# A query weight loaded in 16 + 112 partitions, and the final wait put ahead of the branch, in a decode kernel

## The chip, the core and the metric

The kernel runs on one core of a Trainium2 chip. What is measured is the time of one execution on the device, in microseconds (us), and the median of several executions counts. For the kernel before, three runs gave 1286.26, 1286.32 and 1286.26 us.

## What is computed

One token passes a block with attention and a feed-forward network side by side. Both start from the same normalized input, and both results are added to the input.

```python
xn = _layernorm(x)                                   # x: 1 x 1 x 640
q  = (xn @ wq).reshape(1, 1, 32, 128)                # wq: 640 x 4096
scores = einsum("bhqd,bhkd->bhqk", q, k) * 128**-0.5 # k, v: 1 x 32 x 32768 x 128
o  = einsum("bhqk,bhkd->bhqd", softmax(scores), v)
A  = o.reshape(1, 1, 4096) @ wo                      # wo: 4096 x 640
B  = (silu(xn @ w_gate) * (xn @ w_up)) @ w_down      # hidden width 1728
return x + A + B
```

All inputs are bfloat16. The caches of keys and values hold 32 heads with 32,768 positions of 128 numbers each, 8.39 MB for each of the 64 tensors (K and V of each head); they make up nearly all of the 554 MB that the kernel reads.

## The kernel before

**Buffers.** SBUF holds a ring of three slots, each 64 KB in every partition (`ring`, `SLOTS = 3`). The units of work pass through it in a fixed order: wq, K of head 0, K of head 1, V of head 0, K of head 2, V of head 1, and so on, V of head 31 last, then the feed-forward weights, then wo. Unit number n uses slot n mod 3. So wq lies in slot 0, K of heads 0 and 1 in slots 1 and 2, and V of head 0 is the first unit that takes a slot over, wq's.

**Loads.** All large loads are issued by SyncE (lines 231 to 253). Each has 128 partitions as its rows: partition p takes the p-th contiguous piece of the tensor in HBM, 65,536 bytes for K or V and 40,960 bytes for wq. Before SyncE issues a load into a slot that was used, it waits until the engine that reads the slot is done: L231 and L240 wait for TensorE's work on the unit before. SyncE is a queue in program order. A load's semaphore rises by 16 when all of it has landed.

**The start.** The helper `ahead` moves an instruction that was just added to the program's first basic block in front of the drain that its engine executes ahead of the entry barrier. It's used for wq (SyncE, L158) and for the row x (ScalarE, L159), so that these two loads are issued before the engines pass the barrier and branch to their own blocks. In their blocks, TensorE and VectorE work out the layernorm (lines 286 to 295 and 538 to 558) and leave the normalized input, repeated over 128 columns, in `xnb`. TensorE then waits for `xnb` and for wq (L297 and L298) and computes q for all heads with 40 matrix products (L301). ScalarE copies q to SBUF (L485). SyncE waits for TensorE's eight q steps ahead of V of head 0.

**The main part.** For each head VectorE multiplies K by q in place (L577), TensorE sums the products in groups (L310), VectorE reduces and finds the maximum, ScalarE takes the exponential (L503), and TensorE multiplies the weights by V (L342, L358). The work on V of one head lies between steps of the next head.

**The end.** The last V and wo come in pieces with a semaphore each. TensorE multiplies by the gate, up, down and wo weights (L424, L435, L451), VectorE and TensorE turn the result into 20 rows of 32 numbers (`orow`), and SyncE, having waited for `s_fin`, stores it (L256). After the store, SyncE leaves its block: it branches to the program's final basic block. `body.close()` at the end of the function creates that block; the next line empties it of what the block's exit put there, and L648 then puts one instruction into it, SyncE's wait for the store's semaphore `s_out`. So SyncE branches while the store is under way, and waits after that.

Of the kernel before, what the change touches and what calls it, by code (L numbers as in the profile page):

```python
# [12 lines left out]
def bass_parallel_sum__gqa_block_cached__swiglu_ffn__decode_kernel(  # L13
# [18 lines left out]
    NCD = D // 128  # L32
# [47 lines left out]
    with ExitStack() as es:  # L80
# [3 lines left out]
        def sem(name):  # L84
            return es.enter_context(nc.semaphore(name))
# [34 lines left out]
        s_x, s_wq, s_out = sem("x"), sem("wq"), sem("o")  # L120
# [18 lines left out]
        wq = flat[:, WQ_S * CE:WQ_S * CE + NCD * H * DH]  # L139
# [7 lines left out]
        def ahead(start):  # L147

            at_start = nc.main_func.blocks[0]
            n = len(at_start.instructions)  # L150
            start()
            ins = list(at_start.instructions)
            new = ins[n:]
            drain = next(i for i, x in enumerate(ins)
                         if x.engine == new[0].engine and type(x).__name__ == "InstDrain")
            at_start.instructions = ins[:drain] + new + ins[drain:n]

        ahead(lambda: nc.sync.dma_start(wq, A_wq.rearrange("(p c) n -> p (c n)", c=NCD)).then_inc(s_wq, 16))  # L158
        ahead(lambda: nc.scalar.dma_start(xrow, A_x[0, 0:1, :]).then_inc(s_x, 16))  # L159
        body = ExitStack()  # L160
        block = body.enter_context(nc.Block(no_gpsimd_drain=True))
        f0 = FFN_S * CE
        wg = flat[:, f0:f0 + NCD * F]
        wu = flat[:, f0 + NCD * F:f0 + 2 * NCD * F]
# [22 lines left out]
        def kv_src(cache, h, j0, n):  # L187
            return cache[0, h].rearrange("(p j) d -> p (j d)", p=128)[:, j0 * DH:(j0 + n) * DH]
# [20 lines left out]
        with nc.psum_tensor("ps8", [128, 8, 512], F32) as ps8:  # L209
# [11 lines left out]
            @block.sync  # L221
            def sp(e):
                owner = {}
                for u in units:
                    s = slot_of[u]
                    if s in owner:
                        e.wait_ge(*owner.pop(s))
                    if u[0] == "wq":
                        owner[s] = (s_q, NQB)
                    elif u[0] == "k":  # L230
                        e.dma_start(ring[:, s, :], kv_src(A_k_cache, u[1], 0, NJ)).then_inc(s_slot[s], 16)  # L231
                        owner[s] = (s_qk, NHF * (u[1] + 1))
                    elif u == LASTV:
                        j = 0
                        for i, n in enumerate(TAIL):
                            e.dma_start(ring[:, s, j * DH:(j + n) * DH],
                                        kv_src(A_v_cache, u[1], j, n)).then_inc(s_tail[i], 16)
                            j += n
                    elif u[0] == "v":
                        e.dma_start(ring[:, s, :], kv_src(A_v_cache, u[1], 0, NJ)).then_inc(s_slot[s], 16)  # L240
                        owner[s] = (s_pv, u[1] + 1)
                    elif u[0] == "ffn":
                        e.dma_start(wg, B_w_gate.rearrange("(p c) n -> p (c n)", c=NCD)).then_inc(s_ffn[0], 16)
                        e.dma_start(wu, B_w_up.rearrange("(p c) n -> p (c n)", c=NCD)).then_inc(s_ffn[1], 16)
                        e.dma_start(flat[:, d0:d0 + FM * D], B_w_down[0:FM * 128, :].rearrange(
                            "(p j) n -> p (j n)", j=FM)).then_inc(s_ffn[2], 16)
                        e.dma_start(wdr, B_w_down[FM * 128:F, :].rearrange(
                            "f (t n) -> (f t) n", t=2)).then_inc(s_ffn[2], 16)
                    else:
                        wo_src = A_wo.rearrange("(p j) n -> p (j n)", j=OC)  # L250
                        j = 0
                        for i, n in enumerate(WTAIL):
                            e.dma_start(wo[:, j * D:(j + n) * D], wo_src[:, j * D:(j + n) * D]).then_inc(s_wo[i], 16)  # L253
                            j += n
                e.wait_ge(s_fin, 2)
                e.dma_start(out[0, 0:1, :].rearrange("o (r m) -> (o r) m", m=32), orow[:, :]).then_inc(s_out, 16)  # L256

            @block.gpsimd
            def pool(g):
# [21 lines left out]
            def pe(t):  # L281
# [13 lines left out]
                t.matmul(misc[:, 1:2], lhsT=ones[:, :], rhs=st[:, 2:3], start=True, stop=True).then_inc(s_pa, 1)  # L295

                t.wait_ge(s_a, 11)  # L297
                t.wait_ge(s_wq, 16)  # L298
                with t.Fori(0, NQB) as b:
                    for c in range(NCD):  # L300
                        mm = t.matmul(banks[:, bass.ds(b * 512, 512)], lhsT=xnb[:, c, :],  # L301
# [341 lines left out]
                v.wait_ge(s_or, 1)  # L643
                v.tensor_copy(out=orow[:, :], in_=orow_ps).then_inc(s_fin, 1)

        body.close()
        nc.main_func.blocks[-1].instructions = []
        nc.sync.wait_ge(s_out, 16)  # L648


# [26 lines left out]
```

## Time and profile before

| quantity | value |
|---|---|
| median of three runs | 1286.26 us |
| the profiled execution | 1286.26 us |
| its span, first to last instruction | 1284.9 us |
| mean granted TensorE clock | 0.889 |
| TensorE matrix products busy | 1042.9 us, 81% |
| VectorE busy | 672.2 us, 52% |
| ScalarE busy | 52.1 us, 4% |
| bytes read from HBM | 553.99 MB |
| bytes over the span | 431 GB/s |

The span runs from the issue of wq at 0.00 us to the end of the final wait at 1284.9 us; the 1.36 us between the span and the execution's time lie outside of the instructions that the profile records. "Busy" is the time in which an engine executes instructions, and the DMA's share is the mean over the core's 16 DMA engines. In the timeline a line gives the start in us, the duration in us, the engine (SPq is SyncE's queue, PE TensorE, DVE VectorE, ACT ScalarE), the source line, the operation, and in brackets the idle time ahead of it with what ended it. For a DMA the duration is the time of issuing it; when it lands is told in the table of DMA issues. The trace also records every single DMA packet, here one for each row of a load, with its start, its duration and its bytes.

### The profile page before, as it was taken

The numbers are of one execution on the slowest core, as the hardware profiler recorded it, in microseconds if no ns is written. First come the engines' busy times: TensorE is split into PE (matmuls) and PEld (weight loads), VectorE is DVE, ScalarE is ACT, GpSimd is POOL, SyncE is SP. The second block draws the span as 40 slices with busy tenths as digits, with TensorE's granted clock in tenths as the row PEclk, the third lists the DMA queues.
The fourth block names the chain that finished last, engine by engine and source line by source line (L and its number), as shares of the span: only waits on it lengthen the run. The fifth ranks groups of instructions, "written<-read, shape, count | busy, mean of one in ns | idle before, by whom it ended". The sixth has DMA issues, their size and how long they took to land.

```text
span 1284.9 us, 10032 instructions
## 1 busy us (share of the span) xinstructions
PE 1042.9 (81%) x5160; PEld 261.2 (20%) x3240; DVE 672.2 (52%) x409; ACT 52.1 (4%) x139; POOL 2.6 (0%) x18
## 2 busy tenths in 40 slices
PE   3599777789787798778798877898787798778797
PEld 1021112221112221112221112221112221112227
DVE  0855665445664446664446664446654446654451
ACT  2000000000000000000000000000000000000000
POOL 0000000000000000000000000000000000000000
PEclk9799888898888898888998888998888998888995
DMA  9999999999999999999999999999999999999998
GB/s 424 424 441 433 430 431 441 428 433 433 437 433 428 445 426 435 428 441 428 433 443 428 433 430 441 428 433 435 435 433 430 443 426 435 433 437 433 428 427 370
DMA packets 10987, 554.16 MB, mean 431 GB/s; under 512 B 1247, under 2 KB 1504, under 8 KB 1760
## 3 DMA queue, kind: packets, MB, share of 16 engines
q1 hardware_dynamic: 10974, 554.00, 99.8%
q8 instruction: 9, 0.15, 0.0%
q14 instruction: 2, 0.02, 0.0%
q10 hardware_dynamic: 2, 0.00, 0.0%
HBM read 553.99 MB, written 0.00 MB: 431 GB/s over the span
## 4 chain that ended last, share of the span: by engine, by line
DMA 53%; PE 29%; DVE 12%; issue 5%; SPq 0%; DVEq 0%
DMA ring<-in_A_k_cache_dram 51%; PE ps L358 16%; DVE ring L577 12%; PE ps L310 10%; DMA ring<-in_A_wo_dram 2%; PE ps L342 1%; PE ps L329 1%; PE ps L400 0%; PE ps L394 0%; PE ps L388 0%; PE ps L451 0%; SPq L253 0%; DVEq L577 0%; DVE sc L583 0%; DVE pmax L589 0%
## 5 line engine op out<-in xcount | busy, mean ns | idle before, releaser
L577 DVE TENSOR_TENSOR ring<-ring,qb 128x8192 bf16<-128x8192 bf16 x128 | 557.8, 4421 | 314.9 <-DMA ring<-in_A_k_cache_dram 314.9
L310 PE MATMUL ps<-ring,ident 128*128 128x512 bf16 x1920 | 499.6, 419 | 0.0
L358 PE MATMUL ps<-ring,P 128*4 128x512 bf16 x1920 | 429.0, 379 | 0.0
L329 PE MATMUL ps<-ring,ident 128*128 128x512 bf16 x128 | 56.1, 439 | 218.5 <-DVE ring L577 217.9
L358 PEld LDWEIGHTS ps<-ring,P 128*4 128x4 bf16 x1920 | 158.2, 85 | 230.1
L329 PEld LDWEIGHTS ps<-ring,ident 128*128 128x128 bf16 x128 | 12.6, 99 | 617.0 <-DVE ring L577 357.3
L583 DVE TENSOR_REDUCE sc<-ps 128x64 f32<-128x512 f32 x128 | 82.3, 685 | 64.0 <-PE ps L310 64.0
L595 DVE TENSOR_SCALAR negb<-ps 128x1 f32<-128x1 f32 x32 | 5.1, 159 | 108.4 <-PE ps L400 108.4
L503 ACT ACTIVATE P<-sc,negb 128x256 bf16<-128x256 f32 x32 | 16.2, 507 | 957.2 <-DVE negb L595 957.2
L592 DVE TENSOR_REDUCE m<-ps 1x1 f32<-1x128 f32 x32 | 8.9, 278 | 85.2 <-PE ps L394 85.2
L380 PEld LDWEIGHTS ps<-identf,o 4*128 4x128 f32 x248 | 30.7, 190 | 13.1 <-issue 13.1
L380 PE MATMUL ps<-identf,o 4*128 4x1 f32 x248 | 33.3, 251 | 0.0
L388 PEld LDWEIGHTS ps<-rsum,ones 128*128 128x128 f32 x64 | 12.1, 190 | 100.1 <-issue 99.2
L494 ACT ACTIVATE o<-ps,rzb 4x512 f32<-4x512 f32 x31 | 21.0, 677 | 6.3 <-PE ps L345 6.3
L301 PE MATMUL ps<-ring 128*128 x40 | 10.3, 425 | 11.4 <-DMA ring<-in_A_wq_dram 11.4
L499 ACT ACTIVATE ocol<-ps 128x1 f32 (+1 forms) x31 | 5.4, 173 | 222.4 <-PE ps L380 222.4
L342 PE MATMUL ps<-ring,P 128*4 x64 | 14.3, 379 | 0.0
L589 DVE TENSOR_REDUCE pmax<-sc 128x1 f32<-128x256 f32 x32 | 13.4, 420 | 0.0
L394 PE MATMUL ps<-identf,pmax 128*1 128x128 f32 x64 | 12.2, 272 | 1.2 <-DVE pmax L589 1.2
L400 PE MATMUL ps<-m,ones 1*128 1x1 f32 x64 | 12.1, 256 | 0.4 <-DVE m L592 0.4
L400 PEld LDWEIGHTS ps<-m,ones 1*128 1x128 f32 x64 | 9.4, 183 | 14.0 <-issue 13.3
L565 DVE RECIPROCAL rzb<-ps 128x1 f32<-128x1 f32 x32 | 5.1, 158 | 8.1 <-PE ps L388 8.1
(75 smaller groups left out, 97.2 us busy)
## 6 DMA issues: line engine op xcount, KB each, us to landing
ring<-in_A_v_cache_dram SPq DMA_DIRECT2D x2, 4096.0 KB, 36.5
ring<-in_A_wq_dram SPq DMA_DIRECT2D x1, 5120.0 KB, 15.6
ring<-in_A_wo_dram SPq DMA_DIRECT2D x3, 1280.0 KB, 24.2
ring<-in_B_w_gate_dram SPq DMA_DIRECT2D x1, 2160.0 KB, 22.6
ring<-in_B_w_up_dram SPq DMA_DIRECT2D x1, 2160.0 KB, 27.5
ring<-in_B_w_down_dram SPq DMA_DIRECT2D x1, 2080.0 KB, 31.2
ring<-in_A_wo_dram SPq DMA_DIRECT2D x1, 800.0 KB, 28.3
ring<-in_A_k_cache_dram SPq DMA_DIRECT2D x32, 41.5
```

The lines of the kernel that those rows point to most:

```text
L310: return t.add_instruction(mybir.InstMatmult(start_tensor_calc=False, stop_tensor_calc=stop, tile_size=(128, 128), tile_position=(0, 0), l ...
L329: t.matmul(ob, lhsT=ident[:, :], rhs=src, start=True, stop=False)
L342: t.matmul(O, lhsT=P[:, h % PR, bass.ds(b * (RUN * W) + j, W)], rhs=flat[:, bass.ds(b * (RUN * W * DH) + (s * CE + j * DH), W * DH)], star ...
L358: mm = t.matmul(O, lhsT=P[:, h % PR, j:j + W], rhs=ring[:, s, j * DH:(j + W) * DH], start=(j == 0), stop=(j + W == NJ))
L380: mm = t.matmul(fold_ps, lhsT=o4[:, m * DH:(m + 1) * DH], rhs=identf[0:W, m:m + 1], start=(m == 0), stop=(m == W - 1))
L394: t.matmul(misc[0:1, 0:128], lhsT=pmax[:, h % SR:h % SR + 1], rhs=identf[:, :], start=True, stop=True).then_inc(s_t, 1)
L400: t.matmul(misc[:, 128:129], lhsT=ones[0:1, :], rhs=m1[0:1, h % SR:h % SR + 1], start=True, stop=True).then_inc(s_b, 1)
L494: a.activation(out=o4[:, :], in_=O, func=ACTF.Copy, scale=rzb[0:W, h % SR:h % SR + 1]).then_inc(s_o4, 1)
L503: a.activation(out=P[:, h % PR, :], in_=sc[:, :], func=ACTF.Exp, bias=negb[:, h % SR:h % SR + 1], scale=c_scale, accum_out=rsum[:, h % SR: ...
L577: v.tensor_tensor(out=kh, in0=kh, in1=q[:, None, :].to_broadcast([128, HF, DH]), op=ALU.mult).then_inc(s_mul, 1)
L583: v.tensor_reduce(out=sc[:, i * HF:(i + 1) * HF], in_=bank[i].rearrange("p (j e) -> p j e", e=G), axis=AX.X, op=ALU.add).then_inc(s_red, 1)
L589: v.tensor_reduce(out=pmax[:, h % SR:h % SR + 1], in_=sc[:, :], axis=AX.X, op=ALU.max).then_inc(s_max, 1)
```

## The change

The change has two parts. The first: wq is loaded with two DMAs in place of one, partitions 0 to 15 and partitions 16 to 127, both ahead of the entry barrier and both on SyncE's queue with the same semaphore, so that TensorE waits for 32 in place of 16. The second: SyncE's wait for the output store is moved from the final block to the end of SyncE's own block, so that SyncE waits first and branches afterwards; the final block is then left empty.

```diff
-        ahead(lambda: nc.sync.dma_start(wq, A_wq.rearrange("(p c) n -> p (c n)", c=NCD)).then_inc(s_wq, 16))
+        wq_src = A_wq.rearrange("(p c) n -> p (c n)", c=NCD)
+        for a, b in ((0, 16), (16, 128)):
+            ahead(lambda: nc.sync.dma_start(wq[a:b, :], wq_src[a:b, :]).then_inc(s_wq, 16))
         ahead(lambda: nc.scalar.dma_start(xrow, A_x[0, 0:1, :]).then_inc(s_x, 16))
-        body = ExitStack()
-        block = body.enter_context(nc.Block(no_gpsimd_drain=True))
+        block = es.enter_context(nc.Block(no_gpsimd_drain=True))
...
                 e.dma_start(out[0, 0:1, :].rearrange("o (r m) -> (o r) m", m=32), orow[:, :]).then_inc(s_out, 16)
+                e.wait_ge(s_out, 16)
...
                 t.wait_ge(s_a, 11)
-                t.wait_ge(s_wq, 16)
+                t.wait_ge(s_wq, 32)
...
-        body.close()
-        nc.main_func.blocks[-1].instructions = []
-        nc.sync.wait_ge(s_out, 16)
+    nc.main_func.blocks[-1].instructions = []
```

## The prediction

> **What bounds the kernel now.** I read the page's queue and DMA lines first, then the table of DMA issues, the SyncE waits, and last the timeline of the start and of the end, because the change touches only these two places.
>
> The page, transfers:
> ```profile
> DMA packets 10987, 554.16 MB, mean 431 GB/s; under 512 B 1247, under 2 KB 1504, under 8 KB 1760
> ...
> q1 hardware_dynamic: 10974, 554.00, 99.8%
> ```
> SyncE's queue keeps the 16 DMA engines busy for 99.8% of the span. The trace's packet records say how: a 40,960 B row of wq takes 1.514 us and a 65,536 B row of K or V 2.42 us on its engine, 27.05 GB/s in both, and 16 x 27.05 = 433 GB/s. 554.00 MB / 16 / 27.05 GB/s = 1280.0 us of the 1284.9 us span. So each DMA engine is a full line of work; a microsecond that an engine loses anywhere is not won back later.
>
> The page, issues (KB each where it is the same, us from issue to landing):
> ```profile
> ring<-in_A_wq_dram SPq DMA_DIRECT2D x1, 5120.0 KB, 15.6
> ...
> ring<-in_A_k_cache_dram SPq DMA_DIRECT2D x32, 41.5
> ring<-in_A_v_cache_dram SPq DMA_DIRECT2D x31, 36.8
> ```
> A K or V load is 8.39 MB, 19.5 us at 431 GB/s. It lands 36.8 to 41.5 us after its issue, so 17 to 22 us of other loads stand ahead of it when it is issued: the queue doesn't run dry.
>
> The waits of SyncE (us in total, times, longest):
> ```profile
> SPq L240 <- PE ps L310: 707.3, 30, 24.1
> ...
> SPq L240 <- PE ps L301: 24.1, 1, 24.1
> ...
> SPq L648 <- DMA out_dram<-orow: 0.9, 1, 0.9
> ```
> The second line is V of head 0, which needs wq's slot; the third is the final wait of the program.
>
> The timeline's start:
> ```profile
> 0.00 0.41 SPq L158 DMA_DIRECT2D ring<-in_A_wq_dram  x1
> ...
> 1.06 1.13 SPq L231 DMA_DIRECT2D ring<-in_A_k_cache_dram  x2
> ...
> 5.67 0.82 DVE L558 COPY ring<-xn 128x640 bf16<-128x640 bf16 x1
> ...
> 15.97 10.30 PE L301 MATMUL ps<-ring 128*128 x40 [11.37 <-DMA ring<-in_A_wq_dram]
> ...
> 26.30 0.33 SPq L240 DMA_DIRECT2D ring<-in_A_v_cache_dram  x1
> ```
> PE waits 11.37 us for wq while its other operand is ready at 6.49. What matters more for the end: K of heads 0 and 1 queue behind wq on the same engines, so a slow wq pushes the whole stream. And the timeline's end:
> ```profile
> 1281.43 1.46 PE L451 MATMUL ps<-ot,ring 128*128 128x1 bf16 x40 [0.73 <-DMA ring<-in_A_wo_dram]
> ...
> 1283.40 0.18 DVE L644 CAST orow<-ps 20x32 bf16<-20x32 f32 x1 [0.29 <-PE ps L476]
> 1283.61 0.39 SPq L256 DMA_DIRECT2D out_dram<-orow  x1
> ```
> The last products wait for wo, the last load of the stream; from there to the store 2.2 us of work follow, then the 0.9 us wait of L648 and nothing else.
>
> [...] the store of 20 rows wrote its semaphore from 10 engines[...]. So 16 rows should go one to each engine, and 112 rows seven to each. [...] The trace: SyncE's barrier wait ends at 0.991 us and L231 starts at 1.059, 68 ns with the branch between.
>
> **The change part by part.** The sum is made on the profiled execution: 1286.26 us, of which the span is 1284.90 and 1.36 lie outside; that equals the median.
>
> *One more DMA issue on SyncE at the start.* Second issues in a row take 0.43 us here (L244, L245). SyncE's drain of the entry barrier moves from 0.46 to about 0.93 us, done at 1.05 where ScalarE's was the last at 0.82; all engines enter their blocks some 0.23 us later, and K of head 0 and 1 are issued that much later. Cover: K's first packets start at 13.84 us, when wq's end; the layernorm has 15.56 - 6.49 = 9 us. Cost 0; without cover 0.23.
>
> *First data.* Wq's first packets start 1.09 us (first engine) to 2.23 us (last) after the issue begins; the 20-row store's start 0.81 us after its issue begins. A 16-row issue may start its engines earlier: between 0 and the whole spread of wq's landings, 1.37 us (14.19 to 15.56). I take -0.3 (1.09 - 0.81). If ports bind, as below, most of it is lost in the port's line.
>
> *The 16 rows.* Before, each engine's first row cost one row time, 1.514 us. If four engines share each of four ports, four rows pass one port: 4 x 1.514 = 6.06 us[...]. Loss on every engine 3 x 1.514 = 4.54 us[...]. [...]
>
> *The 112 rows.* Seven consecutive rows to each engine is my estimate[...]. Engine 0 then has rows 16 to 22, engine 8 rows 72 to 78[...]. Seven row times become nine on the engines that meet most often (8 with 13, then again 8 with 13; 1 with 6 twice), seven on those that don't meet: +3.0 us at the worst. Engines that are done go on to K, each on its own port, and there they hold up the late ones, by up to another two row times, 3.0 us. Since every load is waited for until its last engine lands, the worst engine counts: +4.5 + 3.0 = 7.6 to +4.5 + 6.0 = 10.6 us. Repeating the walk with the engines' starts staggered as in the trace gives 6.5 to 11.4, mean 9.1. I take +9. Bounds: 0 if the 112 rows are dealt by port; +31.8 (7 x 3 x 1.514) if they are dealt row by row, because then all 16 engines always sit on four ports.
>
> *What follows from a late wq.* Wq lands at about 24.6, q is done at about 35 (10.3 us of L301) and V of head 0 is issued then and not at 26.30. Ahead of it the engines have K of heads 0 and 1, until 53 plus the delay, so at least 20 us cover remain. Cost 0. PE's wait for 32 in place of 16 has nothing behind it that could have gone ahead. K of head 0 lands later by the delay of its worst engine, and so does all after it: the cost passes to the end undiminished.
>
> *The end.* The wait of L648 ends at 1284.88 either way; the branch is now behind it. [...]bound above by an instruction fetch (1.02 to 1.47 us in the records of queue 8) if the target isn't at hand; SyncE has some 80 instructions in all, so I take 0.06.
>
> Sum: 1286.26 + 9.0 + 0.06 = 1295.3 us, the -0.3 being inside the port's line.
>
> **The rivals.** *A, the forecast, 50%:* ports bind and the seven rows are consecutive: 1291.5 to 1298. For it: the 10 engines of the store[...]. Against it: no small load in the trace.
>
> *B, 14%:* ports bind, the 112 rows are spread well: only the first row is lost, 1286.26 + 4.54 + 0.06 = 1290.9.
>
> *C, 12%:* ports bind, rows are dealt in turn: 8 steps of 4 row times for 8 row times, 24 x 1.514 = 36 us, less what a stagger eases (23 to 38 in the walk): 1309 to 1324.
>
> *D, not slower, 21%:* the ports don't limit, because four engines writing into one port still move 27 GB/s each, or the rows are dealt by port even in the small load. Place: the first row of each engine. Then only the earlier start and the branch remain: 1286.26 - 0.3 + 0.06 = 1286.0; with the whole landing spread gained 1284.9, still within 0.2%. It decides if the first rows' packets take about 2 to 2.6 us, as now, and not 6. For it: in before the first packets' 2.04 to 2.59 us are plain latency.
>
> *E, 3%:* an unforeseen gain over 2.6 us; I see no stage that has one, as start and end together hold 1.1 us before the first packet and 1.4 us outside the span.
>
> **How the numbers follow.** About 0.2% (2.6 us) is what a measurement of this kernel can tell from no change. A, B and C are slower: 0.76; D is the same: 0.21; E faster: 0.03. The time is A's, 1295.3. The range holds A, B and D and leaves out C and E, 15%: 1285.9 to 1299. A's own range is 1291.5 to 1298.
>
> **What would show it.** In the changed profile: 16 packets of 40,960 B that take about 6 us where they took 2.0 to 2.6; a DMA rate near 110 GB/s from 1 to 7 us and well under 430 until about 22 us; L301 starting at 23 to 27 us in place of 15.97; V of head 0 issued at 33 to 37; a landing of K of head 0 about 9 us later; L648 at the same distance from L256. I am wrong if wq lands near 15.6 (then D), near 20 (B), or near 40 to 50 (C); and if wq is late but the span isn't, the queue had slack that I don't see.

## The result, and the profile after

The changed kernel takes 1298.78 us in the median of four executions (1298.68 to 1299.03), against 1286.26 us before: a ratio of 1.0098, 95% interval 1.008 to 1.0115, 12.5 us slower. The profiled execution took 1298.79 us, 1297.3 us of it in the span.

The page of before, bytes moved:

```profile
GB/s 424 424 441 433 430 431 441 428 433 433 437 433 428 445 426 435 428 441 428 433 443 428 433 430 441 428 433 435 435 433 430 443 426 435 433 437 433 428 427 370
```

The page of the changed kernel, bytes moved and the queue, then the two loads that wq consists of now (KB, us from issue to landing):

```profile
GB/s 259 449 423 437 433 427 439 428 441 428 430 438 428 445 424 430 438 428 445 428 430 436 432 438 428 436 432 430 438 428 438 430 430 438 428 441 428 430 428 362
...
q1 hardware_dynamic: 10990, 554.00, 99.7%
...
ring<-in_A_wq_dram SPq DMA_DIRECT2D x1, 4480.0 KB, 27.0
...
ring<-in_A_wq_dram SPq DMA_DIRECT2D x1, 640.0 KB, 8.8
```

The row of GB/s has 40 equal slices of 32.4 us. Only the first one fell, from 424 to 259 GB/s; from the second on the loads run about as before. But the queue's share of the span is still 99.7%: a packet that takes longer counts as busy time for all of it, and the first rows of wq now take 4.25 to 5.05 us where they took 1.54 to 2.59. Had the reader looked at the share alone, nothing would have shown. The 640 KB load of 16 partitions lands after 8.8 us; the other part was issued at 0.45 us and lands 27.0 us later, at 27.5. Before, all of wq was there at 15.6.

The timeline of the changed kernel's start:

```profile
0.00 0.86 SPq L160 DMA_DIRECT2D ring<-in_A_wq_dram  x2
...
1.27 1.09 SPq L232 DMA_DIRECT2D ring<-in_A_k_cache_dram  x2
...
6.94 0.82 DVE L560 COPY ring<-xn 128x640 bf16<-128x640 bf16 x1
...
27.87 11.01 PE L303 MATMUL ps<-ring 128*128 x40 [22.00 <-DMA ring<-in_A_wq_dram]
...
38.91 0.33 SPq L241 DMA_DIRECT2D ring<-in_A_v_cache_dram  x1
...
46.97 4.42 DVE L579 TENSOR_TENSOR ring<-ring,qb 128x8192 bf16<-128x8192 bf16 x1 [39.21 <-DMA ring<-in_A_k_cache_dram]
```

TensorE waits 22.00 us for wq in place of 11.37; V of head 0 is issued at 38.91 in place of 26.30; K of head 0 has its last landing at 46.85 in place of 34.89 us. The end of the same timeline:

```profile
1293.82 1.46 PE L453 MATMUL ps<-ot,ring 128*128 128x1 bf16 x40 [0.72 <-DMA ring<-in_A_wo_dram]
...
1295.78 0.18 DVE L646 CAST orow<-ps 20x32 bf16<-20x32 f32 x1 [0.29 <-PE ps L478]
1295.99 0.37 SPq L257 DMA_DIRECT2D out_dram<-orow  x1
```

and SyncE's last wait. In the trace the branch itself carries it; L80 is the `with` statement at whose end SyncE leaves its block:

```profile
SPq L80 <- DMA out_dram<-orow: 0.9, 1, 0.9
```

From the last products to the store there are 2.2 us, as before, and the wait is 0.9 us, as before. The loss is made at the start and carried to the end.

The semaphore records of both traces say how it is carried. Difference of the last landing, after minus before: wq 11.94 us, K of head 0 11.96, V of head 31 11.89, the gate weights 11.89, the up weights 11.79, the down weights 11.77, wo's first piece 12.36, wo's last piece 12.38; the span 12.38. So 11.9 us come from wq, nothing is won or lost over 64 loads of 8.4 MB, and some 0.5 us are added among the last loads, between the down weights and wo. The other 0.15 us lie outside the span.

### The profile page after: what moved, and what is told of

Its sections match the earlier page's. It is cut to its first block, busy times and chain, and to the rows that moved or that the text cites. A ratio compares the mean times of both kernels' runs of the same rounds, so it can differ in the third digit from the quotient of the medians.

```text
span 1297.3 us, 10033 instructions
## 1 busy us (share of the span) xinstructions
PE 1038.6 (80%) x5160; PEld 261.3 (20%) x3240; DVE 672.2 (52%) x409; ACT 52.1 (4%) x139; POOL 2.6 (0%) x18
## 3 DMA queue, kind: packets, MB, share of 16 engines
q1 hardware_dynamic: 10990, 554.00, 99.7%
## 4 chain that ended last, share of the span: by engine, by line
DMA 53%; PE 28%; DVE 12%; issue 6%; DVEq 0%; SPq 0%
DMA ring<-in_A_k_cache_dram 51%; PE ps L360 16%; DVE ring L579 12%; PE ps L312 9%; DMA ring<-in_A_wo_dram 2%; PE ps L344 1%; PE ps L331 1%; PE ps L402 0%; PE ps L396 0%; PE ps L390 0%; PE ps L453 0%; SPq L254 0%; DVEq L579 0%; DVE sc L585 0%; DVE pmax L591 0%
## 5 line engine op out<-in xcount | busy, mean ns | idle before, releaser
L312 PE MATMUL ps<-ring,ident 128*128 128x512 bf16 x1920 | 493.0, 415 | 0.0
L331 PE MATMUL ps<-ring,ident 128*128 128x512 bf16 x128 | 56.0, 438 | 222.8 <-DVE ring L579 222.2
L591 DVE TENSOR_REDUCE pmax<-sc 128x1 f32<-128x256 f32 x32 | 13.4, 420 | 0.0
L303 PEld LDWEIGHTS ps<-ring 128*128 128x128 bf16 x40 | 4.4, 111 | 28.2 <-issue 24.9
```

Of the source, the lines that this page charges most:

```text
L312: return t.add_instruction(mybir.InstMatmult(start_tensor_calc=False, stop_tensor_calc=stop, tile_size=(128, 128), tile_position=(0, 0), l ...
L331: t.matmul(ob, lhsT=ident[:, :], rhs=src, start=True, stop=False)
L591: v.tensor_reduce(out=pmax[:, h % SR:h % SR + 1], in_=sc[:, :], axis=AX.X, op=ALU.max).then_inc(s_max, 1)
```

## The experiments

### One part of the change at a time

Wq in one load again, with only the wait ahead of the branch:

```diff
-        for a, b in ((0, 16), (16, 128)):
-            ahead(lambda: nc.sync.dma_start(wq[a:b, :], wq_src[a:b, :]).then_inc(s_wq, 16))
+        ahead(lambda: nc.sync.dma_start(wq, wq_src).then_inc(s_wq, 16))
...
-                t.wait_ge(s_wq, 32)
+                t.wait_ge(s_wq, 16)
```

> Wq in one DMA of 128 partitions again; only SyncE's final wait stays ahead of the branch. All theories put the loss on the split, so the time should be 1286.2 to 1286.5 us and wq land at 15.6 us. If the end carries more than the branch's 0.06 us, the excess over 1286.26 is its price; 0.15 us would also explain why more time lies outside the span of the changed kernel than before (1.51 against 1.36 us).

Measured: 1286.40 us against 1286.35 for before on the same chip, ratio 1.0001 (0.9992 to 1.001). Its timeline:

```profile
0.00 0.41 SPq L159 DMA_DIRECT2D ring<-in_A_wq_dram  x1
...
15.48 10.34 PE L302 MATMUL ps<-ring 128*128 x40 [10.89 <-DMA ring<-in_A_wq_dram]
```

The moved wait costs nothing that these runs resolve. Wq even landed 0.48 us earlier in this execution than in that of before (15.07 against 15.56), and the end didn't follow; the last section shows where this gain was lost.

The opposite, the split alone with the end as before:

```diff
-        ahead(lambda: nc.sync.dma_start(wq, A_wq.rearrange("(p c) n -> p (c n)", c=NCD)).then_inc(s_wq, 16))
+        wq_src = A_wq.rearrange("(p c) n -> p (c n)", c=NCD)
+        for a, b in ((0, 16), (16, 128)):
+            ahead(lambda: nc.sync.dma_start(wq[a:b, :], wq_src[a:b, :]).then_inc(s_wq, 16))
```

> Wq in 16 + 112 partitions, the final wait behind the branch as before. The time should be the changed kernel's less the branch: 1298.6 to 1298.8 us; wq's two parts land near 8.8 and 27.5 us. If it is under 1297 us the end of the program has a price that I don't see.

Measured: 1298.58 us, ratio 1.0094 (1.0077 to 1.0111), wq complete at 27.50 us. The split makes the loss. Outside the span lie 1.41 us here and 1.42 with the moved wait alone, against 1.36 before and 1.51 with both; so neither part accounts for those 0.15 us.

### Two loads of the same sizes, cut along the rows

```diff
-        for a, b in ((0, 16), (16, 128)):
-            ahead(lambda: nc.sync.dma_start(wq[a:b, :], wq_src[a:b, :]).then_inc(s_wq, 16))
+        n8 = NCD * H * DH // 8
+        for a, b in ((0, n8), (n8, 8 * n8)):
+            ahead(lambda: nc.sync.dma_start(wq[:, a:b], wq_src[:, a:b]).then_inc(s_wq, 16))
```

> Wq again in two DMAs of the same sizes as in the change, 640 KB and 4480 KB, but cut along the rows: all 128 partitions with the first eighth of their columns, then all 128 with the rest. If the loss comes from the choice of partitions (ports, or which rows are read at the same time), none is left: 1286.0 to 1286.6 us, wq complete near 15.6 us. If two DMAs in themselves cost (a second issue, a gap between them on each engine), 1288 us or more and wq later by the same amount.

Measured: 1286.45 us, ratio 1.0001 (0.9992 to 1.0009). Its DMA issues, to be held against those of the changed kernel:

```profile
ring<-in_A_wq_dram SPq DMA_DIRECT2D x1, 4480.0 KB, 14.7
...
ring<-in_A_wq_dram SPq DMA_DIRECT2D x1, 640.0 KB, 4.6
```

The same bytes in the same two sizes land after 4.6 and 14.7 us in place of 8.8 and 27.0. Neither the second issue nor the small first load costs; the choice of partitions does. Nor does a small first load bring anything: wq is complete at 15.16 us, and the time is that of before.

### Other cuts by partitions

Each is the changed kernel with other bounds in the `for` of the split: `((0, 64), (64, 128))`, `((0, 112), (112, 128))` and `((0, 32), (32, 128))`.

> The change with wq cut into 64 + 64 partitions in place of 16 + 112. [...] 8 rows of 3.03 to 3.2 us in place of 8 of 1.514: 12.1 to 13.5 us more than before, 1298.4 to 1299.8 us. If it is the smallness of the first load that costs, and not the ports, this cut is nearer to before: under 1292.

> The change with the sixteen partitions last: 0 to 111, then 112 to 127. Ports: the same meetings in another order, 17 us for the 112 rows and 4 to 5 us for the 16, against 12.1 in one load: 1297 to 1299 us. If the cost comes from being first (a cold start with one row per engine), it is gone here: under 1290.

> The change with 32 + 96 partitions. Coupled theory: the 32 rows take two steps of 3.03 to 3.2 us with all ports in use doubled, the 96 rows six steps with two or three ports doubled, 2.8 to 3.06 us each: wq is complete 10.8 to 12.7 us later than before and the time 1297.5 to 1299.5 us. Free theory (only the engines that meet are slow): the 96 rows cost as the walk says, mean 6 us, 1292 to 1297 us.

| cut | time, us | ratio (95%) | wq complete at, us |
|---|---|---|---|
| one load (before) | 1286.26 | 1 | 15.56 |
| 16 + 112 (the change) | 1298.78 | 1.0098 (1.008 to 1.0115) | 27.50 |
| 64 + 64 | 1299.66 | 1.0104 (1.0075 to 1.0134) | 28.22 |
| 112 + 16 | 1297.86 | 1.009 (1.0061 to 1.012) | 26.32 |
| 32 + 96 | 1298.63 | 1.0095 (1.0065 to 1.0124) | 27.00 |

Every cut by partitions costs 11.6 to 13.4 us, in either order and with halves too. It isn't the small load, and it isn't the cold start. In the last three rows K of head 0 lands 0.76 to 0.85 us later still than wq does (13.42, 11.62 and 12.29 us behind before, and wq 12.66, 10.77 and 11.45), so the time moves by more than the last column. With halves the packets show 3.2 us per row nearly throughout, about twice the 1.514 us of before: in the terms of the next runs, the pace of two writers on every port in use.

### Loads measured by themselves: the port

In a copy of the kernel before, loads from wq go into free parts of the ring ahead of all else, each waited for before the next is issued. This set and the two after it were executed once each; the load of 128 rows that opens each set took 15.10, 15.30 and 15.28 us. Two loads as examples:

```diff
+        ahead(lambda: nc.sync.dma_start(spare[0:16, :], wq_src[0:16, :]).then_inc(s_pr, 16))
+        ahead(lambda: nc.sync.wait_ge(s_pr, 32))
+        ahead(lambda: nc.sync.dma_start(spare[0:106:7, :], wq_src[0:16, :]).then_inc(s_pr, 16))
+        ahead(lambda: nc.sync.wait_ge(s_pr, 48))
```

> Ahead of the kernel before, loads from wq into a free part of the ring, each waited for before the next is issued; the results of the kernel don't depend on them. Issue to landing, less about 2 us of latency, in row times of 1.514 us for 40,960 B. Ports theory (a port of SBUF takes 27 GB/s, whoever writes): 128 rows 8; 16 rows into partitions 0 to 15: 4; the same 16 source rows into partitions 0, 7, ..., 105[...]: 2; sixteen source rows 0, 7, ..., 105 into partitions 0 to 15: 4; partitions 0, 4, ..., 60 (8 ports): 2; four rows into partitions 0 to 3 (one port): 4, into 0, 4, 8, 12 (four ports): 1; 112 rows alone: 9; the same rows as seven DMAs that give engine e row 16 + 7e + i: also 9 if the DGE deals consecutive rows; 32 rows: 4; 64 rows: 8. Memory theory (the rows that are read at the same time lie on few HBM channels): the destination doesn't matter, so 16 consecutive source rows take the same long time into any partitions, and the spread source rows 0, 7, ..., 105 are quick into partitions 0 to 15 as well. The third, that any engine away from its own port is slow whatever the others do: four rows into four ports slow too, and all loads but the one of 128 rows slower by one factor. The pair 16 + 112 should show what the changed kernel shows, some 22 to 26 us.

"DGE" in the expectation stands for what deals a load's rows out to the engines. SyncE's timeline in this kernel. The start of one line minus that of the line before is the time from issue to landing of the load before; L179 to L185, and L193 with L194, are issued together and count from the first issue:

```profile
0.00 0.40 SPq L161 DMA_DIRECT2D ring<-in_A_wq_dram  x1
15.10 0.35 SPq L163 DMA_DIRECT2D ring<-in_A_wq_dram  x1
23.29 0.62 SPq L165 DMA_DIRECT2D ring<-in_A_wq_dram  x1
28.43 0.34 SPq L167 DMA_DIRECT2D ring<-in_A_wq_dram  x1
36.26 0.51 SPq L169 DMA_DIRECT2D ring<-in_A_wq_dram  x1
...
47.30 0.30 SPq L173 DMA_DIRECT2D ring<-in_A_wq_dram  x1
54.69 0.66 SPq L175 DMA_DIRECT2D ring<-in_A_wq_dram  x1
58.90 0.33 SPq L177 DMA_DIRECT2D ring<-in_A_wq_dram  x1
79.63 0.55 SPq L179 DMA_DIRECT2D ring<-in_A_wq_dram  x1
...
144.40 0.31 SPq L193 DMA_DIRECT2D ring<-in_A_wq_dram  x1
144.75 0.42 SPq L194 DMA_DIRECT2D ring<-in_A_wq_dram  x1
171.79 0.35 SPq L196 DMA_DIRECT2D ring<-in_A_wq_dram  x1
```

Worked out of these starts, and of those of the lines left out:

| line | load | us |
|---|---|---|
| L161 | 128 rows | 15.10 |
| L163 | source rows 0 to 15 into partitions 0 to 15 | 8.19 |
| L165 | the same source rows into partitions 0, 7, ..., 105 | 5.15 |
| L167 | source rows 0, 7, ..., 105 into partitions 0 to 15 | 7.82 |
| L169 | source rows 0, 7, ..., 105 into the same partitions | 5.47 |
| L171 | source rows 0 to 15 into partitions 0, 4, ..., 60 | 5.58 |
| L173 | four rows into partitions 0 to 3 | 7.39 |
| L175 | four rows into partitions 0, 4, 8, 12 | 4.20 |
| L177 | 112 rows into partitions 16 to 127 | 20.73 |
| L179 to L185 | the same as seven loads of 16 rows, 16 + i, 23 + i, ... | 20.26 |
| L187 | 112 rows into partitions 0 to 111 | 19.94 |
| L189, L191 | 32 rows; 64 rows, from partition 0 | 8.94; 15.63 |
| L193, L194 | 16 + 112 rows, as in the change | 27.39 |

The destination decides, not the source: L163 and L165 read the same bytes, L163 and L167 write the same partitions. That fells the memory theory. The third theory, distance from the own port, wanted one slow factor for every load but the one of 128 rows; L163 and L165, sixteen rows each, differ by 3.0 us. A port stands here for what some partitions share when rows are written to them. Which of them share is read from the times. Four rows into partitions 0 to 3 take 7.39 us and the same four into 0, 4, 8, 12 take 4.20: 0 to 3 are one port. Sixteen rows into 0, 4, ..., 60, no two of them in the same four, still take 5.58, 1.38 more than L175, so some fours seem to share as well. Which of them do isn't in the records; the walk of the prediction took it as given. What distance alone costs is left to the next set, which has a second choice of four ports. Eight row times and 3.0 us of latency make the 15.10 us of L161; 32 rows at two writers per port should take 2 x 2 row times + 3.0 = 9.1 (8.94 measured), 64 rows 15.1 (15.63). Single rows look somewhat cheaper than four row times, since part of the latency lies beside them; in the second set three loads of 16 rows into partitions 0 to 15 in a row took 6.02 us for each second row and nearly each third, 4 x 1.51.

The pair L193 and L194 takes 27.39 us, 12.29 longer than one load of 128 rows; in the changed kernel wq took 27.50, 11.94 longer than before. By difference it comes apart: the 112 rows alone take 20.73 in place of 7 x 1.514 + 3.0 = 13.6, so 7.1 us too long, and 4.1 longer than the nine row times of the walk's slowest engine (9 x 1.514 + 3.0 = 16.6); the 16 rows add the rest, 4.8 us in the changed kernel and 5.2 in the pair.

That the seven loads of L179 to L185, which give engine e row 16 + 7e + i, take as long as the one of 112 rows fits consecutive sevens; rows dealt in turn would have meant 42 us (7 x 6.02). And the packet records of L177 show all engines in step, row after row (us, four of the 16 engines that can be followed through):

```
engine seen first at   row 1  2     3     4     5     6     7
59.855                 3.10   2.87  2.10  1.80  2.87  2.88  2.84
60.086                 2.99   2.86  2.03  1.80  2.89  2.87  2.65
60.368                 1.78   2.82  2.55  1.83  2.53  2.89  2.89
60.890                 1.74   2.85  2.35  1.80  2.83  2.87  2.71
ports doubled          2      2     1     1     2     2     2
```

The last line is the walk's and not a record: how many ports have two writers when all engines are at that row. Where one is doubled, the rows take about 1.8 to 2.5 us; where two are, mostly about 2.8, on every engine, those with a port to themselves included. The walk let these run at 1.514. So the walk's map fits, and something holds up engines that don't meet.

### What holds up the others

> Probes ahead of the kernel before, as in the first set; the results of the kernel don't depend on them. Two theories for why the 112 rows took 17.7 us and not the 13.6 us of my walk. Free theory (the walk): an engine whose port no other engine writes at that time runs at 1.514 us per 40,960 B row, whatever happens elsewhere. Coupled theory: a port with two writers holds up all engines that run beside it. Three times 16 rows into partitions 16, 23, ..., 121 (two ports doubled, by engines 0 with 5 and 8 with 13): free: 12 engines at 1.51 us for their second and third row, four at 3.03; coupled: all at about 2.8. The same from partition 19 (one port doubled, engines 7 and 12): free: 14 engines at 1.51, two at 3.03; coupled: all at 1.8 to 3.0. Four rows into partitions 0 to 3 (one port, engines 0 to 3), then 128 rows: free: 12 engines at 1.51 from the start; coupled: they are slow until engines 0 to 3 have left the port, some 4.5 us. Controls: the same with four rows into 0, 4, 8, 12[...]: 1.51 in both theories, and with two rows in place of four. Four rows into 16, 20, 24, 28 (single writers[...]): 1.51 in both, more if distance from the own port costs by itself. Three times 16 rows into partitions 0 to 15: 6.06 each. 64 + 64 rows: 8 rows of 3.03 to 3.2, 27 to 28.6 us from issue to landing.

SyncE's timeline in the second set of probes (three loads each from L164 and L168 on, pairs from L180 to L190):

```profile
15.30 0.63 SPq L164 DMA_DIRECT2D ring<-in_A_wq_dram  x1
...
27.11 0.51 SPq L168 DMA_DIRECT2D ring<-in_A_wq_dram  x1
...
38.26 0.71 SPq L172 DMA_DIRECT2D ring<-in_A_wq_dram  x1
...
45.55 0.58 SPq L176 DMA_DIRECT2D ring<-in_A_wq_dram  x1
...
52.84 0.30 SPq L180 DMA_DIRECT2D ring<-in_A_wq_dram  x1
...
72.84 0.60 SPq L183 DMA_DIRECT2D ring<-in_A_wq_dram  x1
...
89.35 0.25 SPq L186 DMA_DIRECT2D ring<-in_A_wq_dram  x1
...
106.61 0.61 SPq L189 DMA_DIRECT2D ring<-in_A_wq_dram  x1
...
122.66 0.33 SPq L192 DMA_DIRECT2D ring<-in_A_wq_dram  x1
```

L164 (two ports doubled) takes 11.81 us and L168 (one port doubled) 11.15: nearly the same, because each is waited for until its slowest engine lands. The packets tell them apart. In L164 the second and third rows take 3.05 to 3.12 us on nearly all 16 engines; in L168 they take 1.514 us on twelve and up to 1.9 on another two, and 2.5 to 3.0 on the two that meet. Neither theory was right in both. L176 (four rows into 16, 20, 24, 28) takes the same 7.29 us as L172 (into 0, 4, 8, 12), and in both the second and third rows take 1.51 to 1.54 us. Whichever port is an engine's own, it isn't at it in both, if the two loads are dealt alike; so distance showed no cost, and the third theory falls. L180, four rows into one port and then 128, takes 20.0 us against 16.51 for its control L183.

> A third set of probes ahead of the kernel before: a few rows on the lowest engines, then 128 rows at once, to see what holds up engines that share no port. Count theory: one port with two writers holds up nobody else, two such ports or more than two writers on one hold up all 16. Then, for the first row of the engines that have no part in the meeting (about 2.2 us with latency when free): rows into 0, 2, 4, 6[...]: 3 to 4 us; into 2, 4, 6, 8 (one port doubled): 2.2, free; into 0, 1, 2 (three writers on one port): 3 to 5; into 0, 4, 8, 12: 2.2, free; into 0 to 7 (two ports with four writers): 5 or more; into 0, 2, ..., 14 (four ports doubled): 3 to 4. Pair theory (it is particular engines that share a way, here 0 with 5 and 8 with 13): the first and the last are free too, since engines 0 to 3 and 0 to 7 don't meet in those pairs. The 112 rows alone once more: 20 to 21 us, all engines in step, with short rows in the fourth place (1.8 us) where one port only is doubled.

First rows of those engines that have no part in the meeting, from the packet records of the second and third sets:

| a few rows first, into partitions | who meets | first row of the others, us: range (median) |
|---|---|---|
| 0, 4, 8, 12 (control, second set) | nobody | 1.7 to 2.5 (2.21) |
| 0, 4, 8, 12 (control, third set) | nobody | 1.5 to 2.8 (2.39) |
| 0, 1 | two on one port | 1.6 to 2.5 (2.10) |
| 2, 4, 6, 8 | two on one port | 1.5 to 2.6 (2.28) |
| 0, 1, 2 | three on one port | 1.8 to 2.5, then 1.7 to 1.9 for the second |
| 0, 2, 4, 6 | two on each of two ports | 2.5 to 3.4 (2.92) |
| 0, 2, ..., 14 | two on each of four ports | 2.4 to 2.8 (2.61) |
| 0 to 3 | four on one port | 4.5 to 5.7 (5.13) |
| 0 to 7 | four on each of two ports | 4.8 to 4.9 (4.84) |

One port with two writers left the others alone (medians 2.10 and 2.28 us, controls 2.21 and 2.39). Two such ports slowed them, also where other engines meet than in the 112 rows (0, 2, 4, 6: median 2.92 us), so the pair theory falls, as far as one execution shows. Four writers on one port brought everyone to about its pace (5.13 and 4.84 us). The four doubled ports of 0, 2, ..., 14 were expected at 3 to 4 us and stay inside the range of the third set's control: that row shows nothing. Three on one port came out milder than expected: the others' first rows are free and the second ones slightly slow. So the count theory holds in outline, with the bound at three writers wrong; L164 and L168 above are its clearest case. The time of a whole kernel agrees: 32 + 96 took 1298.63 us, where the coupled theory said 1297.5 to 1299.5 and the free one 1292 to 1297. What it is in the chip that holds the others up isn't shown.

## Why the prediction was right, and where it was short

The sign, the place and the cause, ports that are shared, were right; how far the sharing reaches was not. The time came out 0.8 us above the range that forecast A gave itself (1291.5 to 1298) and 0.2 us inside the whole range, so the 112 rows below were nearly too much for it.

**The entry.** The second issue took 0.41 us (0.43 forecast), K's issue moved by 0.21 us (0.23), and nothing waited for it. In the profiled execution the row x also landed 1.39 us later (2.78 in place of 1.39; with the split alone it came at 1.37), which moved the layernorm's last copy from 5.67 to 6.94 us; wq came 20 us after that.

**The first data.** No gain: the first packet starts at 1.03 us in place of 1.09. Cutting along the rows, where no port gets in the way, brought nothing at the end either.

**The 16 rows.** +4.54 us forecast; 4.8 is what the 112 rows leave of wq's delay in the changed kernel, 5.2 in the pair measured ahead of the kernel, and 6.02 - 1.51 = 4.51 for such rows in a row. Right, and for the stated reason: the records of the changed kernel show 16 packets of 40,960 B that take 4.25 to 5.05 us (about 6 forecast), one to each engine by the 16 writes to the load's semaphore from 7.22 to 8.82 us.

**The 112 rows.** This is the term that was mis-sized. +4.5 us was taken, and +6.0 was the most in the walk with equal starts; it measured 7.1. The walk takes the engines through their seven rows step by step and lets those that meet at a port share it equally. No trace stood behind its order of the rows and its map of the ports when it was made; the pattern of the seven steps fits both. Wrong was its rule that an engine with a port to itself runs on at full rate. With two ports doubled all 16 do about 2.8 us per row here (3.05 to 3.12 in L164), and five of the seven steps have two: 5 x about 1.3 + 2 x about 0.3 to 0.6 above 1.514 makes some 7 us.

**The way to the end.** V of head 0 was issued at 38.91 us, with K of heads 0 and 1 still ahead of it; the delay of wq stood unchanged in the last V, 11.89 of 11.94 us. That step is right, and the later marks follow from the mis-sized term: TensorE starts on wq at 27.87 us (23 to 27 forecast), and V's issue was forecast for 33 to 37.

**The end.** The branch behind the wait was put at 0.06 us, an estimate next to the 68 ns that the trace of before has with a branch between; one load with the moved wait measured 0.05 us above before, inside its interval of -1.0 to +1.3 us. The forecast's sum lacks another 0.5 us that appears between the down weights and wo's first piece. There the last engine lands 2.50 us after the first (1.88 before). The split alone shows the same step (a spread of 2.39, and a delay that goes from 11.81 to 12.39 us). The other cuts don't: they have their whole delay by K of head 0 and end within 0.12 us of it. Which engine is hit there, and by what, stays open.

So 9.06 us were forecast and 12.5 came: +0.3 in the 16 rows, +2.6 in the 112 rows, +0.5 at the end. Of the rivals, B (a well spread rest) would have been 1290.9 us, C (rows dealt in turn) at least 1309, D (ports that don't limit) 1286.0; the packets of 4 to 5 us exclude D, the pace of the 112 rows B and C.

## What to carry to other kernels

Where the DMA engines are the bound, cut a load along its rows and keep all 128 partitions in every piece, which cost nothing here (1286.45 us); a cut by partitions slowed wq here from 371 GB/s, from its first packet's start to its last one's end, to 204 with 16 + 112 and 201 with halves. The share of busy DMA, 99.7% here, doesn't show such a loss; GB/s by slices and the time to landing do. When a load into few partitions is priced, a port with four writers (5.13 and 4.84 us for the others' first row) or two ports with two each (2.92, and about 2.8 per row in the 112 rows) has to be charged to all engines, not only to those that meet there; one port with two writers (2.10 and 2.28, controls 2.21 and 2.39) held up nobody else.

## What the runs showed of the hardware that was not expected

- Engines that write to a port of their own are held up by others: 3.05 to 3.12 us per row on nearly all 16 engines with two ports doubled, 1.514 on most with one.
- Small gains at the start get lost before the end. With wq complete 0.48 us earlier the last V landed only 0.05 us earlier and the time was the same. The loads are 0.49 us ahead of before up to 73 us, and at the next landing, 93 us, they are 0.12 us behind; with the cut along the rows 0.38 us are lost at the same place. Between the two landings the trace has a fetch of 16 KB of instructions, at 77 us, 1.0 us long. Three more, of 1.0 to 1.1 us, follow up to 206 us. Before the first fetch the spread between the first and the last engine of a load is constant, and with the next load it steps up: from 1.37 to 1.60 us in before (1.90 after the second fetch), from 0.91 to 1.75 with the moved wait alone, from 0.65 to 2.01 with halves; the last engine is what every load is waited for. That these fetches are what sets the spread was not tried.
